# Left-over rows of two heads side by side in the matrix array, in an attention and mixer kernel with a planned order

## The chip, the core and the metric

The kernel runs on one core of one Trainium2 chip. Its metric is the device time of one execution in microseconds. The engines are TensorE (PE; its weight loads are listed apart as PEld), VectorE (DVE), ScalarE (ACT), GpSimd (POOL) and SyncE (SP), which here only issues transfers. Each engine works through its own queue in order, and waits for the others by semaphores.

## The reference

Attention over 4 batches, 8 heads, 576 rows and 64 columns a head, with a bias computed from row and column numbers, then a token mixer and a channel mixer on the result:

```
scores = (1/8) q @ k^T + bias            # bias[h,i,j] from log1p(|i-j|) / log1p(max(i,1)) through a 32-wide layer
attn   = exp(scores - max) / (sum + 1e-9)
x      = (attn @ v), heads side by side  # 4 x 576 x 512
u      = x + (relu(x^T @ w_tok1) @ w_tok2)^T
out    = u + relu(u @ w_ch1) @ w_ch2
```

## The kernel before

Numbers of high precision are split into a high and a low half, and a product is made of three: high x high, high x low, low x high. The program has three stages.

1. The bias table is computed (products of `mm`, L521, overwritten to SBUF by `over`, L526) and written to DRAM in 36 pieces.
2. Sixteen units follow, each one pair of heads (`hp`, 4) of one batch (`b`, 4), in the order of the list `units`. A unit has five query chunks (`c`). Chunks 0 to 3 hold 128 rows of one head after the other; chunk 4 holds the left-over 64 rows of both heads, the first head on partitions 0 to 63 and the second on 64 to 127. For each chunk: `scores` (L799; in chunks 0 to 3 the two heads run on the two row halves of the array), `biased` (L808, bias and maximum on VectorE), `numer` (L821, exponential on ScalarE), then the transposition of the result, by TensorE (`flip`, L850, with halves by L853 and L856) or, for the first third of chunks 0, 2 and 4, by a transposing transfer from SP (`turn`, L839), ahead of which ScalarE makes the high half (`rest_hi`, L831) and GpSimd the low (`rest_lo`, L835 and L389). `back` (L877 to L879) multiplies with v: 30 matmuls of 64 or 65 columns a chunk, the 65th being the sum. `norm1` to `norm3` (L889, L892, L902) divide by the sum. After the chunks `mix1` and `mix2` (L921 to L932) do the token mixer for that pair, and the rows are stored to DRAM (L950 for chunks 0 to 3, L952 for the left-over rows).
3. The channel mixer reads the rows back: first-layer products (L1112 to L1114), second-layer products (L1203 to L1205) and, for the later blocks, products of sums of quarters (L1297 to L1299).

In chunk 4 before, each transposed block has 128 columns, of which 64 are wanted. So the transposed tiles have margins of 64 zero columns on both sides (cleared by `fillt`, L619), the weights are read 64 columns to the left or right, and each of the two heads' results lands on all 128 partitions, of which the half for that batch (`r`) is kept. Even batches use the upper half of a shared tile of left-over rows, odd ones the lower, so the mixer's weights for the last rows (`wt1`) are laid out twice.

What sets the order: nothing is issued in the order of the source. Every step is added to a `Plan` with its possible engines and their costs in microseconds, a due time (from the table `DUE`) and the steps it follows. `Plan.order` simulates the engines with these costs and takes, of the steps that could start first, the one due earliest. `wire` costs stand for transfers; `LAT["D"]` is added behind one. Where TensorE would stand still for over `GAP`, warming matmuls (`keep_warm`, L323; 128 weight columns, 256 columns, result unused) are written ahead of the waiting step, as many as fit in the planned gap at 0.11 each. The queue of each engine is the order in which the plan issues.

The bias of a head pair is read back chunk by chunk (`bias_load`, L725 and L728) into one of two slots. The reads for pairs 2 and 3 overwrite those of pairs 0 and 1, and wait for all `biased` steps of that pair.

Of the kernel before, what the change touches and what calls it, by code (L numbers as in the profile page):

```python
# [56 lines left out]
ON = {'dlo': {'P': 1.9},  # L57
      'dlo2': {'P': (1.9, 2361.48), 'V': (0.67, 1106.04)},
      'late': {'P': (0.7, 2182.65), 'A': (0.58, 1929.34)},
      'klow': {'P': (1.5, 725.99), 'V': (0.83, 1661.39)},  # L60
      'zlow': {'P': (1.25, -2146.14), 'V': (0.6, 1553.62)},
      'twhole': {'P': (2.4, -4606.89), 'V': (1.21, -877.53)},
      'tsum': {'P': (3.0, 1929.59), 'V': (1.72, -1684.06)},
      'tlow': {'P': (2.1, 1515.55), 'V': (1.15, 1987.78)},
      'oall': {'P': (2.7, 2055.41), 'V': (1.2, 3109.89)},
      'norm': {'V': (0.35, -1885.6), 'A': (0.88, -688.24)},
      'over': {'A': 0.65, 'V': (0.72, 542.69)},
      'vh': {'P': (0.7, 5132.87), 'V': (0.4, -2850.86), 'A': (0.6, -3115.7)},
      'vl': {'P': (1.36, 3857.78)}}
DUE = {'tie': 5203.01,  # L70
       'blk': -1054.62,
       'blkn': 61.65,
       'rect': -611.01,
       'bmm': -2320.58,
       'over': -3195.14,
       'put': -4039.31,
       'bl': -239.81,
       'bln': 58.76,
       'sums': 1668.2,
       'sumsn': 550.06,  # L80
       'measw': 331.87,
       'measwn': 95.35,
       'amax': 338.6,
       'scales': 76.3,
       'scalet': -3035.39,
       'scalec': -965.86,
       'fill': -1626.0,
       'fill1': 540.27,
       'tok': -1994.09,
       'tokn': -250.04,  # L90
       'dec1': -350.27,
       'dec2': 379.95,
       'dec3': -1095.12,
       'dec4': 826.35,
       'dec5': -740.87,
       'load_k': -384.96,
       'load_q': -892.85,
       'split_k': -249.75,
       'first_k': 530.16,
       'first_q': 277.17,  # L100
       'split_q': -616.87,
       'load_v': -2393.38,
       'prep_v': 4942.17,
       'prep_vh': -1513.45,
       'prep_vl': -5395.73,
       'scores': -1907.38,
       'biased': -476.81,
# [1298 lines left out]
```

## Time and profile before

| | us |
|---|---|
| median of 3 runs (627.15 to 627.92) | 627.87 |
| the profiled execution | 630.01 |
| its span, first to last instruction | 627.4 |
| PE busy in the span (98%) | 613.2 |
| DVE busy (77%) | 480.0 |
| ACT busy (65%) | 406.9 |
| POOL busy (48%) | 301.1 |

Matmuls are pipelined: one lasts longer than the distance to the next one's start, so TensorE's busy time counts overlaps once and says little about how dense it is. The distance between starts says more. The stages are, by the lines that run in them: the bias table to about 55 us, the units to about 358 us (first `scores` at 54, last `mix2` at 358), the channel mixer from 350 us to the end.

### The profile page before, as it was taken

What the parts mean: (1) busy time and instruction counts of PE and PEld (TensorE: products, weight loads), DVE (VectorE), ACT (ScalarE), POOL (GpSimd) and SP (SyncE); (2) the same over time, 40 slices, a digit from 0 to 9 for tenths busy, and PEclk for the clock granted to TensorE, in tenths of its full rate; (3) what the DMA queues carried; (4) which work ended last, traced back from release to release, by engine and by line L of the source; (5) the groups of instructions that cost most, each with busy time, mean ns of one, the idle gap of its engine ahead of it and who ended that gap; (6) DMA issues with size and microseconds to landing.
All of it is one profiled execution on the core that took longest, in us unless ns stands there. A gap on an engine that the chain in (4) does not pass through costs nothing.

```text
span 627.4 us, 18139 instructions
## 1 busy us (share of the span) xinstructions
PE 613.2 (98%) x7237; PEld 452.3 (72%) x7237; DVE 480.0 (77%) x1188; ACT 406.9 (65%) x751; POOL 301.1 (48%) x343
## 2 busy tenths in 40 slices
PE   9999998999999999999999999999999999999997
PEld 4346776989988998899898964444444468845886
DVE  7897898988899998998999868985764884355322
ACT  7998887988898899999897535543533641234110
POOL 0006789886686888978665510002335742212211
PEclk9999997999999999999999999999999999999999
DMA  8999778999897965658447999544123015400221
GB/s 311 367 387 357 188 159 193 284 263 217 186 247 208 247 145 142 151 128 203 106 91 134 207 351 241 201 134 135 35 67 93 9 34 135 101 1 1 85 85 33
DMA packets 102339, 104.53 MB, mean 167 GB/s; under 512 B 62192, under 2 KB 71920, under 8 KB 102256
## 3 DMA queue, kind: packets, MB, share of 16 engines
q1 hardware_dynamic: 92608, 82.79, 50.2%
q10 hardware_dynamic: 9648, 20.60, 11.3%
q8 instruction: 56, 0.92, 0.6%
q14 instruction: 27, 0.22, 0.1%
HBM read 68.88 MB, written 20.33 MB: 142 GB/s over the span
## 4 chain that ended last, share of the span: by engine, by line
PE 77%; DVE 8%; ACT 7%; DMA 4%; POOL 2%; issue 2%; ACTq 0%; SPq 0%; POOLq 0%; DVEq 0%
PE pair L799 9%; PE bank L850 7%; PE bank L1112 5%; PE bank L1114 5%; PE bank L1113 5%; PE bank L1299 4%; PE bank L1298 4%; PE bank L1297 4%; PE pair L521 4%; PE pair L1113 2%; PE bank L1205 2%; PE pair L1114 2%; PE bank L1204 2%; PE pair L1112 2%; PE bank L1203 2%; PE bank L877 2%
## 5 line engine op out<-in xcount | busy, mean ns | idle before, releaser
L821 ACT ACTIVATE z<-z,mx 128x576 f32<-128x576 f32 (+1 forms) x119 | 91.1, 778 | 9.4 <-DVE mx L808 8.4
L808 DVE CUSTOM_DVE_ANT_0 z<-pair,slots 128x576 f32<-128x576 f32 (+1 forms) x119 | 89.0, 757 | 6.1 <-PE pair L799 5.5
L856 DVE SCALAR_TENSOR_TENSOR t2a<-bank,t2a 128x384 f16<-128x384 f32 (+1 forms) x134 | 70.8, 536 | 8.2 <-ACT t2a L853 7.3
L850 PE MATMUL bank<-id,z 128*128 128x128 f32 x425 | 68.4, 283 | 2.3 <-ACT z L821 1.0
L853 ACT ACTIVATE t2a<-bank 128x384 f16<-128x384 f32 (+1 forms) x134 | 62.7, 471 | 9.5 <-PE bank L850 5.2
L799 PE MATMUL pair<-kh,qh 64*128 64x288 f32 (+1 forms) x288 | 61.5, 349 | 4.2 <-DVE mx L808 3.7
L1112 PE MATMUL bank<-slots 128*128 128x512 f16 (+1 forms) x168 | 58.6, 349 | 0.0
L1113 PE MATMUL bank<-slots 128*128 128x512 f16 (+1 forms) x168 | 58.6, 349 | 0.0
L1114 PE MATMUL bank<-slots 128*128 128x512 f16 (+1 forms) x168 | 58.6, 349 | 0.0
L1308 DVE SCALAR_TENSOR_TENSOR slots<-bank,crow,slots 128x256 f32<-128x256 f32 x42 | 19.5, 481 | 49.7 <-PE bank L1299 36.2
L877 PE MATMUL bank<-vh,t2a 128*128 128x65 f16 x472 | 53.6, 194 | 0.0
L850 PEld LDWEIGHTS bank<-id,z 128*128 128x128 f32 x425 | 45.7, 141 | 10.8 <-issue 3.4
L878 PE MATMUL bank<-vl,t2a 128*128 128x64 f16 x472 | 53.3, 191 | 0.0
L879 PE MATMUL bank<-vh,t2a 128*128 128x65 f16 x472 | 53.3, 192 | 0.0
L799 PE MATMUL pair<-kl,qh 64*128 64x288 f32 (+1 forms) x288 | 52.1, 301 | 0.0
L799 PE MATMUL pair<-kh,ql 64*128 64x288 f32 (+1 forms) x288 | 50.5, 294 | 0.0
L1242 POOL TENSOR_TENSOR me<-me 128x512 f32<-128x512 f16 x12 | 13.6, 1154 | 68.7 <-DVE wd L1088 68.4
L799 PEld LDWEIGHTS pair<-kh,qh 64*128 64x128 f32 (+1 forms) x288 | 33.9, 187 | 15.5 <-issue 6.4
L877 PEld LDWEIGHTS <-t2a 128*128 128x128 f16 x472 | 43.4, 97 | 0.5 <-issue 0.5
L878 PEld LDWEIGHTS <-t2a 128*128 128x128 f16 x472 | 43.6, 98 | 0.2
L879 PEld LDWEIGHTS <-t2a 128*128 128x128 f16 x472 | 43.4, 97 | 0.0
L1320 POOL TENSOR_TENSOR slots<-slots 128x1024 f32<-128x1024 f32 x6 | 14.1, 2350 | 56.5 <-DVE slots L1308 44.6
(272 smaller groups left out, 2131.9 us busy)
## 6 DMA issues: line engine op xcount, KB each, us to landing
keep<-wc SPq DMA_DIRECT2D x24, 512.0 KB, 4.4
wd<-wc SPq DMA_DIRECT2D x24, 512.0 KB, 5.0
bd<-slots SPq DMA_DIRECT2D x36, 295.5 KB, 6.2
slots<-bd SPq DMA_DIRECT2D x16, 576.0 KB, 7.2
tv<-v ACTq DMA_DIRECT2D x16, 320.0 KB, 3.9
qq<-qT ACTq DMA_DIRECT2D x16, 320.0 KB, 3.6
kk<-kT ACTq DMA_DIRECT2D x16, 320.0 KB, 3.9
z<-vr SPq DMA_DIRECT2D x8, 576.0 KB, 7.3
```

Source lines behind the costliest of these rows:

```text
L799: PE.matmul(out=pairs[both[h].i][:, 512 - i + n * i:512 + n * i], lhsT=qx[x][w, c * 128:c * 128 + 128], rhs=kx[y][w, k0:k0 + i], start=(j ...
L808: V.tensor_tensor_reduce(out=st["z"][z.i][:, o], in0=pairs[ph.i][:, 512 - i:512 + i], in1=bias_m[hp][:, c, h, :] if c < NCH else bias_l[hp ...
L821: A.activation(out=zz, in_=zz, func=ACTF.Exp, bias=mx_t[z.i][:, h:h + 1], scale=-1.0)
L850: PE.transpose(banks[tb.i][:, n * 128:(n + 1) * 128], st["z"][z.i][:, 384 * i + n * 128:384 * i + (n + 1) * 128], id32)
L853: A.activation(out=block(h.i, 0, m), in_=banks[tb.i][:, 0:128 * m], func=ACTF.Copy, scale=P_SCALE)
L856: V.scalar_tensor_tensor(out=block(h.i, 3, m), in0=banks[tb.i][:, 0:128 * m], scalar=P_SCALE, in1=block(h.i, 0, m), op0=ALU.mult, op1=ALU. ...
L877: PE.matmul(out=o, lhsT=lh, rhs=vh[:, n, 0:D + 1], start=(i == 0), stop=False)
L878: PE.matmul(out=ps[:, h, 0:D], lhsT=lh, rhs=vl[:, n, :], start=False, stop=False)
L879: PE.matmul(out=o, lhsT=ll, rhs=vh[:, n, 0:D + 1], start=False, stop=(i == 4))
L1112: PE.matmul(out=ps, lhsT=w[0][:, c], rhs=uh[:, c], start=(c == 0), stop=False)
L1113: PE.matmul(out=ps, lhsT=w[0][:, c], rhs=ul[:, c], start=False, stop=False)
L1114: PE.matmul(out=ps, lhsT=w[1][:, c], rhs=uh[:, c], start=False, stop=(c == 3))
```

## The change

- Chunk 4's product with v: `back` now loads 64 weight columns for each head and writes the first head's rows to partitions 0 to 63 and the second's to 64 to 127 of the same columns; the matmuls of the two heads alternate. The planner's cost for it goes from 0.917 to 0.52.
- The margins of the transposed tiles and their fills go (tiles of 768 instead of 896 columns). Left-over rows of both heads stand on a block diagonal of the x tile, scaled by two instructions (`norm4`) instead of one, stored by two transfers of 64x64 instead of one of 64x128. `wt1` has five blocks instead of six, with the last rows' weights on both partition halves, so its third piece is 256 words wide instead of 512. `wt2`'s last 64 columns are copied once (`twice`) instead of cleared.
- A read of a chunk's bias for pairs 2 and 3 waits for that chunk's `biased` steps only.
- Planned costs of transfers rise (`LAT["D"]` 0.4 to 0.6, k and q 1.06 to 1.25, v 1.18 to 1.4, bias 1.9 to 2.3 behind the first pair, stores 0.75 to 1.1). `GAP` falls from 1.0 to 0.6, warming matmuls are also written where no bank is idle, and `STAY`, `SLACK` and all due times change. `rest_lo` may also go to VectorE; the plan leaves all 48 on GpSimd.

```diff
-LAT = {"V": 0.15, "A": 0.16, "P": 0.08, "T": 0.2, "D": 0.4, "-": 0.0}
-GAP, PAD, PAD_MOST = 1.0, 0.11, 24
-SLACK = 0.096
-STAY = 1604.78
+LAT = {"V": 0.15, "A": 0.16, "P": 0.08, "T": 0.2, "D": 0.6, "-": 0.0}
+GAP, PAD, PAD_MOST = 0.6, 0.11, 24
+SLACK = 0.116
+STAY = 796.12
...
-DUE = {'tie': 5203.01,
-       'blk': -1054.62,
+DUE = {'tie': 4998.17,
+       'blk': -647.68,
...
-                if t - at["T"] > GAP and idle:
-                    s.pad = min(PAD_MOST, int((t - at["T"] - 0.3) / PAD)), min(idle)[1]
+                if t - at["T"] > GAP and (idle or any(h.kind == "pair" for h in s.take)):
+                    s.pad = min(PAD_MOST, int((t - at["T"] - 0.25) / PAD)), min(idle)[1] if idle else None
...
-        fillt = add({"P": 2.6}, DUE["fill1"], lambda e: [G.memset(t[:, a:a + 64], 0.0) for t in st["t2a"] + st["t2d"] for a in (0, 832)], after=[drawn])
...
-            after = [] if hp == 0 else [*bias_all, *wt_s] if hp == 1 else last_use[hp - 2]
-            mask = add({"P": 0.2}, t0, mask_out(hp), after=after)
+            def after(c):
+                return [] if hp == 0 else [*bias_all, *wt_s] if hp == 1 else last_use[hp - 2, c]
+
+            mask = add({"P": 0.2}, t0, mask_out(hp), after=after(NCH))
...
-                    blk = ([(n, n) for n in range(5)], [(n + 1, n) for n in range(4, 9)]) if c < NCH else [[(n + 5 * h, n) for n in range(5)] for h in range(2)]
-                    for h in range(2):
-                        for i, (n, t) in enumerate(blk[h]):
-                            d = 64 * (h - b % 2) if c == NCH else 0
-                            lh, ll = (tt[t][:, y[t] + d:y[t] + d + 128] for y in (th, tl))
-                            o = ps[:, h, 0:D + 1]
-                            PE.matmul(out=o, lhsT=lh, rhs=vh[:, n, 0:D + 1], start=(i == 0), stop=False)
-                            PE.matmul(out=ps[:, h, 0:D], lhsT=lh, rhs=vl[:, n, :], start=False, stop=False)
-                            PE.matmul(out=o, lhsT=ll, rhs=vh[:, n, 0:D + 1], start=False, stop=(i == 4))
+                    if c < NCH:
+                        turns = [[(h, n + h, n, slice(0, 128), i)] for h in range(2) for i, n in enumerate(range(4 * h, 4 * h + 5))]
+                    else:
+                        turns = [[(0, n + 5 * h, n, slice(64 * h, 64 * h + 64), n) for h in range(2)] for n in range(5)]
+                    for turn in turns:
+                        for x, y, d in ((th, vh, D + 1), (th, vl, D), (tl, vh, D + 1)):
+                            for h, n, t, w, i in turn:
+                                PE.matmul(out=ps[w, h, 0:d], lhsT=tt[t][:, x[t] + w.start:x[t] + w.stop], rhs=y[:, n, 0:d],
+                                          start=(i == 0 and x is th and y is vh), stop=(i == 4 and x is tl))
...
+                def norm4(e, hb=hb, hr=hr):
+                    for h in range(2):
+                        q = slice(64 * h, 64 * h + 64)
+                        xo, ps, rc = st["x"][xh_.i][q, 4, q], av_of(hb)[q, 2, 0, 0:D], rc_t[hr.i][q, 2, 0]
+                        if e == "A":
+                            A.activation(out=xo, in_=ps, func=ACTF.Copy, scale=rc)
+                        else:
+                            V.tensor_scalar(out=xo, in0=ps, scalar1=rc, scalar2=None, op0=ALU.mult)
```

Three places show how the queues move. On TensorE, chunk 4 of the first unit's product with v (`rect` and `t2a` hold transposed blocks, `vh` and `vl` the halves of v). Before:

```order
L877 LDWEIGHTS rect_123
L877 MATMUL bank1_67<-vh0_111,rect_123 128x65
L878 LDWEIGHTS rect_123
L878 MATMUL bank1_67<-vl0_112,rect_123 128x64
L879 LDWEIGHTS rect_123
L879 MATMUL bank1_67<-vh0_111,rect_123 128x65
```

After:

```order
L889 LDWEIGHTS rect_123
L889 MATMUL bank0_66<-vh0_111,rect_123 64x65
L889 LDWEIGHTS rect_123
L889 MATMUL bank0_66<-vh0_111,rect_123 64x65
L889 LDWEIGHTS rect_123
L889 MATMUL bank0_66<-vl0_112,rect_123 64x64
L889 LDWEIGHTS rect_123
L889 MATMUL bank0_66<-vl0_112,rect_123 64x64
```

The count of matmuls stays 30; each writes 64 partitions instead of 128, and neighbours are now the same term of the two heads. With this TensorE changes the shape of its tiles 171 times in the whole program, 140 times before.

On GpSimd, the stretch ahead of the first low halves (L835 and L389 before, L846 and L391 after; L733 and L737 are the first of two fills of the bias mask). Before:

```order
L733 MEMSET slots 64x64
L734 MEMSET slots 64x64
L647 TENSOR_TENSOR slots<-keep 128x288
L389 TENSOR_TENSOR kl_108<-kk,kh_107 128x640
L641 TENSOR_SCALAR keep<-keep 128x288
L439 MEMSET vh_111 128x10
L440 MEMSET vh_111 64x1
L441 MEMSET vh_111 64x1
L619 MEMSET t2a_90 128x64 x2
...
L619 MEMSET rect 128x64 x10
L835 TENSOR_SCALAR rect<-rect 128x384
L389 TENSOR_TENSOR rect<-rect 128x384
```

After:

```order
L737 MEMSET slots 64x64
L738 MEMSET slots 64x64
L846 TENSOR_SCALAR z_121<-z_121 128x384
L391 TENSOR_TENSOR rect<-z_121,rect 128x384
L441 MEMSET vh_111 128x10
L442 MEMSET vh_111 64x1
L443 MEMSET vh_111 64x1
```

The low halves move ahead of a split of k, two steps of weight decoding and three fills; the 22 margin fills are gone.

On TensorE, the end of the first run of first-layer products in the channel mixer (L1114 before, L1135 after) and the first second-layer product (L1203 before, L1224 after). Before:

```order
L1113 LDWEIGHTS slots
L1113 MATMUL bank_68<-slots 128x512
L1114 LDWEIGHTS slots
L1114 MATMUL bank_68<-slots 128x512
L1203 LDWEIGHTS slots
L1203 MATMUL bank_69<-me,slots 128x512
```

After:

```order
L1135 LDWEIGHTS slots
L1135 MATMUL bank_67<-slots 128x512
L325 LDWEIGHTS ones_74
L325 MATMUL bank_69<-ones_74 128x256
...
L1224 LDWEIGHTS slots
L1224 MATMUL bank_69<-me,slots 128x512
```

Ten warming matmuls (L325) stand between them. In the whole program there are 148 instead of 85; 18 of either number stand at the start. Of the rest, 67 before and 81 after stand before the last scores of the fourth unit; after that, before has none, and after has 36 in four groups (13, 4, 6 and 13) before the last scores of the fifth unit, 3 in the fourteenth, and these ten.

## Rows read from the trace of the kernel before

**Rows 1.** Busy us (instructions) of each engine by stretch, then clock, DMA share, GB/s.

```profile
55.00:100.00 45.00, 40.35 (x524) 33.51 (x524) 40.87 (x113) 37.40 (x69) 35.82 (x66) 0.99 0.83 206
100.00:160.00 60.00, 59.38 (x938) 54.03 (x939) 51.81 (x138) 51.04 (x99) 46.45 (x55) 0.95 0.97 250
160.00:345.00 185.00, 182.79 (x3168) 166.42 (x3168) 170.11 (x454) 165.76 (x312) 140.23 (x149) 1.00 0.71 164
...
375.00:627.40 252.40, 247.91 (x1523) 148.86 (x1521) 150.28 (x320) 89.91 (x165) 61.55 (x42) 1.00 0.31 88
```

**Rows 2.** Timeline of PE, 205 to 206.6 us: start, us, line, operation, tiles, count.

```profile
205.30 0.29 PE L799 MATMUL pair<-kl,qh 64*128 64x288 f32 x2
...
205.83 0.29 PE L799 MATMUL pair<-kh,ql 64*128 64x288 f32 x2
206.05 0.55 PE L850 MATMUL bank<-id,z 128*128 128x128 f32 x3
206.44 0.19 PE L877 MATMUL bank<-vh,rect 128*128 128x65 f16 x1
206.47 0.20 PE L878 MATMUL bank<-vl,rect 128*128 128x64 f16 x1
```

**Rows 3.** Stretches as in rows 1, around the fall of the clock.

```profile
92.00:99.00 7.00, 5.04 (x67) 3.76 (x65) 6.62 (x22) 5.52 (x11) 6.58 (x7) 1.00 0.71 131
99.00:106.00 7.00, 6.46 (x32) 5.03 (x31) 4.82 (x15) 5.43 (x11) 6.38 (x9) 0.51 1.04 241
```

**Rows 4.** Timeline of PE in the token mixer's first product, 207.7 to 208 us.

```profile
207.71 0.22 PE L921 MATMUL bank<-xh,wt1h 128*128 128x128 f16 x1
...
207.99 0.22 PE L923 MATMUL bank<-xh,wt1l 128*128 128x128 f16 x1
```

**Rows 5.** DVE groups by form: busy us and mean ns of one, then idle before.

```profile
L902 DVE TENSOR_TENSOR x<-bank,rc 64x128 f32<-64x128 f32 x16 | 4.5, 284 | 0.1
...
L889 DVE TENSOR_SCALAR rc<-bank 128x4 f32<-128x4 f32 x16 | 2.4, 153 | 0.3
```

**Rows 6.** Issues of line 952 on SP: ns minimum, median, maximum, first and last start.

```profile
L952 SPq DMA_DIRECT2D ul<-x x16: 461/474/552, 121.9 to 360.6; - x16
```

**Rows 7.** Timeline of POOL ahead of the first transposing transfer.

```profile
59.61 1.05 POOL L619 MEMSET t2a<- 128x64 f16 x12
...
62.02 0.92 POOL L389 TENSOR_TENSOR rect<-rect 128x384 f16<-128x384 f32 x1
```

**Rows 8.** The chain that ended last, 62 to 68 us: start, us, what.

```profile
62.97 4.64 DMA rect<-rect
```

**Rows 9.** The same chain at other places, merged pieces, in order of time.

```profile
55.97 2.18 PE bank L323 x19
...
100.99 1.90 PE pair L799 x6
102.89 1.73 PE bank L323 x8
104.62 1.64 PE pair L799 x12
...
159.63 0.93 PE pair L799 x6
...
209.54 0.55 PE bank L850 x5
...
228.00 0.99 PE pair L799 x12
```

**Rows 10.** Timelines of DVE and of PE at the first second-layer product.

```profile
399.78 0.74 DVE L659 SCALAR_TENSOR_TENSOR me<-wd,sc,me 128x512 f16<-128x512 f32 x1
...
400.36 0.38 PE L1203 MATMUL bank<-me,slots 128*128 128x512 f16 x1
```

**Rows 11.** Timeline of PEld in the bias stage, 49.3 to 51 us.

```profile
49.54 0.30 PEld L521 LDWEIGHTS pair<-slots 128*32 128x32 f32 x20 [0.30 <-issue]
50.15 0.13 PEld L521 LDWEIGHTS pair<-slots 128*32 128x32 f32 x4 [0.30 <-issue]
```

More of the change, by code (lines that the diff above doesn't have):

```diff
@@ new lines @@
+DUE = {'tie': 4998.17,
+       'blk': -647.68,
+       'blkn': 79.22,
+       'rect': -763.01,
+       'bmm': -2389.2,
+       'over': -4044.78,
+       'put': -4260.31,
+       'bl': 687.35,
+       'bln': 124.96,
+       'sums': 2272.7,
+       'sumsn': 556.43,
+       'measw': -241.54,
+       'measwn': 92.23,
+       'amax': -141.77,
+       'scales': -970.88,
+       'scalet': -3014.61,
+       'scalec': 772.49,
+       'fill': -404.22,
+       'fill1': 1011.38,
+       'tok': -2233.95,
+       'tokn': -164.97,
+       'dec1': -585.91,
+       'dec2': -380.29,
+       'dec3': -392.21,
+       'dec4': 699.42,
+       'dec5': -1407.03,
+       'load_k': -1264.93,
+       'load_q': -1001.19,
+       'split_k': -1147.47,
+       'first_k': 1410.2,
+       'first_q': 232.19,
+       'split_q': -402.69,
+       'load_v': -3735.76,
+       'prep_v': 4016.62,
+       'prep_vh': -2553.8,
+       'prep_vl': -4781.38,
+       'scores': -1500.38,
+       'biased': -1240.21,
+       'exp': 519.27,
+       'hi': 533.73,
+       'lo': 972.63,
+       'turn': -190.87,
+       'flip': -1140.85,
+       'fliphi': -1951.26,
+       'flip2': -1141.38,
+       'fliplo': 936.49,
+       'back': 600.3,
+       'norm': -1082.88,
+       'mix0': -1335.11,
+       'mix1': -205.71,
+       'relu': -6606.92,
+       'mix2': -4026.09,
+       'mix2b': -234.02,
+       'store': -125.27,
+       'w1': 1709.14,
+       'w1n': 166.52,
+       'U0': 2578.51,
+       'U0n': -582.54,
+       'U1n': -95.1,
+       'U1': 2259.35,
+       'U2': -1637.7,
+       'Un': 36.54,
+       'U3': 2477.65,
+       'U4': -2877.49,
+       'u1': 4361.86,
+       'u2': -1921.15,
+       'u3': -275.58,
+       'u4': -48.29,
+       'u5': 764.07,
+       'G': 2604.87,
+       'G0': 1101.84,
+       'G0n': 138.28,
+       'g1': -3213.41,
+       'g2': 1156.61,
+       'ur': -60.29,
+       'H': 4157.9,
+       'e1': -456.52,
+       'e2': -4056.91,
+       'e3': 1090.96,
+       'e4': 480.31,
+       't2': 1312.25,
+       't3': 6.7,
+       't4': 631.82,
+       'T1': -1272.87,
+       'Tn': -1.35,
+       'rd': 628.59,
+       'urs': 789.77,
+       'un': -139.24,
+       'v1': -136.69,
+       'v2': 5966.57,
+       'v3': -590.31,
+       'v4': 4843.9,
+       'v5': 1879.7,
+       'v6': 1191.78,
+       'v7': 857.25,
+       'v8': -1948.99,
+       'w2m': -953.59,
+       'w2mn': 105.51}
@@ L1346, in attention_mixer @@
             if s.pad:
[L1347 removed]
+                keep_warm(pairs[0][:, 0:192] if s.pad[1] is None else banks[s.pad[1]], s.pad[0])
             n = nc.n_instructions()
```

213 lines of the change are left out of this document (62 added, 151 removed).

## The prediction

> **What bounds the kernel now.** I read the busy times by stage first [rows 1]. From 375 us to the end TensorE runs a dense stream of long products, and the reader should see that nothing else is near it: VectorE is busy 150.28 of 252.40 us, ScalarE 89.91. Those products exist in the same number after the change, so the end moves only by what the attention stage before it gives or takes, and by what is put between the dense products. In the attention stage no engine is alone. From 160 to 345 us TensorE shows 182.79 of 185 us, but its matmuls overlap in the pipeline, so that figure alone proves little; the starts of neighbours [rows 2] lie as close as they ever do, and that is the better sign. VectorE has 170.11 us there, 92%, ScalarE 165.76, 90%. So TensorE is the first limit and VectorE is 8% behind. From 55 to 100 us TensorE has real holes (40.35 of 45 us), and right after them the granted clock falls to 0.51 [rows 3], which is the 1.2 GHz level.
>
> The profiled execution took 630.01 us, 2.6 more than its span of 627.4; the median of the runs is 627.87. I make the sum inside the span and take it off the median.
>
> **Part 1: left-over rows of two heads side by side.** A unit (one head pair of one batch) has five query chunks; the fifth holds 64 left-over rows of each of two heads. Its product with v is 30 matmuls of 64 or 65 columns before and after; now each loads 64 weight columns, and the two heads' matmuls stand in pairs on the two halves of the array. Before, starts are 0.03 us apart [rows 2], so 30 of them take 0.90 us. The trace has no pair of column halves. The nearest is the scores' pair on two row halves: 288 columns twice, four starts of pairs in 0.53 us, 0.13 each. What would 288 columns cost alone? Matmuls of 128 columns start 0.056 us apart (five in 0.28 [rows 4]) and those of 65 at 0.03, so 0.41 ns a column, and 288 come to 0.12 us; a pair costs some 0.01 us more than one pass. I take 0.040 us for a pair of 65, so 15 pairs are 0.60 us. The array also has to change its shape on the way in and out. Out of the scores' row halves the next start comes 0.22 us later where 0.13 is usual [rows 2], so 0.09 a change, 0.18 for both. Together 0.78 against 0.90: 0.12 us a unit, **1.9 us less** over 16 units. The ends: a pair for the price of one pass (0.030) gives 0.63 and 4.3 us less; halves that don't overlap (0.060) give 1.08 and 2.9 us more. I stay near the row halves because they are the only pairs of large tiles here; both ends stay for the range.
>
> **Part 2: the work beside it.** VectorE's scaling of these rows was one instruction on 64x128 (0.284 us) and becomes two on 64x64 from PSUM. The same kind on four columns takes 0.153 [rows 5]; halfway between the two is 0.22, so 0.44 against 0.284: 0.16 us a unit, 2.5 us in all. VectorE has 8% to spare, and only where it has none does this count: I charge a third, **0.8 us more** (0 to 2.5). The reciprocal loses a column, the last addition works on 128 partitions instead of 64: the partitions work at once, so nothing. Each unit stores its left-over rows by two transfers instead of one: one more issue on SP, about 0.47 us [rows 6], 16 times; the kernel reads those rows back only in the dense stage, and SP waits for data between its issues, so nothing, unless a transpose queued behind the store is what TensorE waits for.
>
> **Part 3: fills that go.** Before, GpSimd cleared the margins of the transposed tiles, 22 fills of which 12 take 1.05 us, 1.9 us together, just ahead of the first low halves [rows 7]; those end at 62.94 us, and the first transposing transfer of the chain starts at 62.97 and holds it for 4.64 us [rows 8]. Now GpSimd does the low halves directly behind the mask fills. What could be late next is ScalarE's high half and VectorE's scale for v, busy in the same moments, so I take **1.0 us less** (0 to 1.8).
>
> **Part 4: the slow clock.** After the holes of 92 to 99 us (TensorE busy 5.04 of 7) the granted clock is 0.51 from 99 to 106 us [rows 3]. Six scores matmuls took 1.90 us there against 0.93 later, twelve 1.64 against 0.99, eight warming matmuls 1.73 where 19 took 2.18 at full clock (0.115 each) [rows 9]: 2.5 us lost. The new order writes 81 warming matmuls into the first four units instead of 67 and in more places, because a gap of 0.6 instead of 1.0 in the planner's count now gets them; so the long hole is less likely. I take **2.0 us less** (2.5 less, or 2.5 more if a second slow stretch appears).
>
> **Part 5: bias reads, dearer transfers, new order.** Reads of the third and fourth head pair may start chunk by chunk. The trace shows no TensorE wait for them in the steady stage, which is dense from 100 us on [rows 1], so nothing. The new costs and due times move nearly everything; the engine that does each kind of work stays the same. One place I can price: ten warming matmuls now stand between the last first-layer product and the first second-layer product of the dense stage. Before, the matmul there starts at 400.36 us without a hole, and the low half of the fourth weight block, wanted nine products later, began on VectorE at 399.78 [rows 10]: little slack. Ten times 0.115 is **1.1 us more**; if the weights are later still, that wait is already in it.
>
> The sum: -1.9 + 0.8 - 1.0 - 2.0 + 1.1 = -3.0 us, so 627.9 - 3.0 = **624.9 us**.
>
> **The rivals.**
> (a) The warming matmuls become the wait (slower). After the fourth unit's scores the new order has four groups of them, 36 in all, where the old had none and TensorE was busy 59.38 of 60 us [rows 1]. With 14 more in the first units and 3 later that is 53, times 0.115: 6.1 us. They are free only while the engine would have stood still. If the transfers come sooner than the planner now believes, they are in the way: 624.9 + 6.1 = 631.0. It turns slower than before once half of them, 3 us, is uncovered. For it: the old trace needed no such gaps. Against it: the other engines work their backlog off meanwhile.
> (b) Loads of 64 columns are slow. A 128-column fp32 load with its transposition takes 0.11 us, five in 0.55 [rows 9]. If a 64-column load goes at that rate, 0.055, and the halves load at once, a chunk is 15 x 0.055 + 0.18 = 1.0 us, 1.7 us more instead of 1.9 less: 628.5. If the halves load one after the other, a chunk is 1.83 us: 641.7. Against the second: 20 loads of 32 columns on column quarters took 0.30 us where four took 0.13, so they start some 0.01 apart [rows 11]. The Trainium skill, TensorEngine Tiling (Array Packing), section Feature Incompatibilities, says column tiling excludes the fast weight load, and its page TensorE: Matmul & The Clock Gate, section LDWEIGHTS, puts a plain load at columns / 1.2 ns, an estimate of 53 ns for 64 columns; by that rule the time is that of the first price. No run yet shows a 64-column fp16 load.
> (c) VectorE becomes the limit. Part 1 then gives nothing and part 2 costs all of its 2.5 us: -1.0 - 2.0 + 1.1 + 2.5 = +0.6, so 628.5. For it: 92% busy; against it: TensorE's holes there are smaller than VectorE's.
> (d) All goes well: pairs at one pass (-4.3), the fills' whole 1.8, the clock's whole 2.5, no charge elsewhere: -8.6, so 619.3.
>
> **How the numbers follow.** Forecast 0.36, (a) 0.18, (b) 0.12 (0.02 of it for the long form), (c) 0.10, (d) 0.24. A measurement of this kernel can tell 0.2%, 1.3 us, from no change: 626.6 to 629.1 counts as the same. The forecast's own range is 622.5 to 627; it gives 0.33 to faster and 0.03 to same. (d) is faster. (b) and (c) lie at the upper edge of the same, 0.12 to it, 0.06 slower, 0.04 faster between their terms. (a) gives 0.03 faster, 0.01 same, 0.14 slower. So faster 0.64, same 0.16, slower 0.20. For 8 in 10 the range goes from 618, a little below (d), to 631, the whole of (a).
>
> **What would show it.** Part 1: starts of the fifth chunk's pairs 0.04 us apart and 0.09 at its edges; 0.06 or 0.11 means (b). Part 3: the first transposing transfer before 62 us. Part 4: a granted clock without a stretch near 0.5. Part 5: the first second-layer product directly behind its warming matmuls. (a) shows as warming matmuls whose next matmul starts without any wait, with its operands long ready; (c) as VectorE without holes in the steady stage while TensorE waits for it. A dense stage of another length, counted from its first product to the end, would make the whole argument wrong.

## The result, and the profile after

The changed kernel takes 631.58 us in the median (630.91 to 631.99) against 627.73; the ratio is 1.0062, interval 1.0049 to 1.0074. I forecast 624.9 (618 to 631) and faster; it is slower by 0.6%. The profiled execution took 631.41 us, its span is 629.6. Of the executions of the kernel before, one took 1006.34 us at a mean granted clock of 0.557 and is left out of every figure here. Engine times of the page, to be held against the table before the change:

```profile
PE 615.1 (98%) x7300; PEld 448.4 (71%) x7300; DVE 481.7 (77%) x1204; ACT 406.1 (64%) x751; POOL 297.6 (47%) x321
```

By stretch, busy us and count of each engine, then clock, DMA share and GB/s, as in [rows 1]:

```profile
55.00:100.00 45.00, 40.91 (x536) 33.74 (x534) 40.04 (x118) 37.95 (x71) 35.94 (x47) 1.00 0.95 244
100.00:160.00 60.00, 59.21 (x957) 52.55 (x954) 52.27 (x142) 49.60 (x93) 40.56 (x49) 1.00 0.97 239
160.00:345.00 185.00, 182.54 (x3186) 163.10 (x3184) 169.82 (x457) 166.16 (x313) 139.72 (x149) 1.00 0.66 154
375.00:629.60 254.60, 249.39 (x1539) 150.06 (x1537) 150.74 (x320) 90.95 (x168) 61.03 (x42) 1.00 0.32 89
```

The reader is to see how little these rows tell. They look like those before, TensorE as busy as ever, and 4 us are gone. Only GpSimd's 40.56 us from 100 to 160 stand out, against 46.45 before. Busy time counts warming matmuls as work, so from here on I count the useful matmuls in a stretch.

The pairs themselves did what was hoped. Timeline of PE in the changed kernel, the fifth chunk of one unit (the answer to [rows 2]):

```profile
201.06 0.55 PE L861 MATMUL bank<-id,z 128*128 128x128 f32 x3
201.54 0.22 PE L889 MATMUL bank<-vh,rect 128*64 128x65 f16 x2
201.59 0.20 PE L889 MATMUL bank<-vl,rect 128*64 128x64 f16 x2
...
202.00 0.20 PE L889 MATMUL bank<-vh,t2a 128*64 128x65 f16 x2
202.13 0.55 PE L861 MATMUL bank<-id,z 128*128 128x128 f32 x3
```

From the first start to the start behind the group it is 0.59 us, where 30 single matmuls took 0.91. In the trace a pair's second matmul starts 0.003 us after its first, and pairs follow each other every 0.032; the first start comes 0.20 after the last transposition where 0.11 is usual, the start behind the group 0.13 after its last instead of 0.03.

The last sign that the prediction named showed too: the dense stage has another length. First products of the dense stage, the kernel before and then the changed one (count, ns minimum, median, maximum, first and last start in us):

```profile
L1112 PE MATMUL bank<-slots x168: 272/379/389, 349.7 to 571.7; 128*128 128x512 f16 x120, 128*128 128x256 f16 x48
L1133 PE MATMUL bank<-slots x168: 272/379/390, 349.7 to 573.5; 128*128 128x512 f16 x120, 128*128 128x256 f16 x48
```

From 349.7 us to the end of the span it is 277.7 us before and 279.9 in the changed kernel. Of these 2.2 us, 1.1 are the ten warming matmuls; 0.7 are a hole at 548 us that the kernel before doesn't have, with a weight load there that waits for its transfer; 0.4 lie behind the last product.

```profile
548.12 0.38 PE L1133 MATMUL bank<-slots 128*128 128x512 f16 x1 [0.34 <-issue]
```

So between these two executions the units differ by 0.4 us only, and the dense stage by 2.2. That is one execution of each; the next section shows how much a stage can differ between executions of one kernel.

### The profile page after: what moved, and what is told of

It is laid out like the page before. It is cut to its first block, busy times and chain, and to the rows that moved or that the text cites. A ratio compares the mean times of both kernels' runs of the same rounds, so it can differ in the third digit from the quotient of the medians.

```text
span 629.6 us, 18331 instructions
## 1 busy us (share of the span) xinstructions
PE 615.1 (98%) x7300; PEld 448.4 (71%) x7300; DVE 481.7 (77%) x1204; ACT 406.1 (64%) x751; POOL 297.6 (47%) x321
## 4 chain that ended last, share of the span: by engine, by line
PE 65%; DVE 7%; POOL 4%; issue 2%; ACT 2%; DMA 0%; ACTq 0%; POOLq 0%; DVEq 0%
PE pair L806 6%; PE bank L1133 5%; PE bank L1134 5%; PE bank L1135 5%; PE bank L889 5%; PE bank L861 4%; PE bank L1319 4%; PE bank L1318 4%; PE bank L1320 4%; PE bank L1224 2%; PE pair L1133 2%; PE pair L1135 2%; PE bank L1225 2%; PE bank L1226 2%; PE pair L1134 2%
## 5 line engine op out<-in xcount | busy, mean ns | idle before, releaser
L829 ACT ACTIVATE z<-z,mx 128x576 f32<-128x576 f32 (+1 forms) x121 | 92.4, 778 | 11.9 <-DVE mx L815 10.6
L815 DVE CUSTOM_DVE_ANT_0 z<-pair,slots 128x576 f32<-128x576 f32 (+1 forms) x121 | 90.4, 758 | 6.2 <-PE pair L806 3.7
L864 ACT ACTIVATE t2a<-bank 128x384 f16<-128x384 f32 (+1 forms) x134 | 62.6, 471 | 14.0 <-PE bank L861 10.2
L1135 PE MATMUL bank<-slots 128*128 128x512 f16 (+1 forms) x168 | 58.6, 349 | 0.0
L889 PE MATMUL bank<-vh,t2a 128*128 128x65 f16 (+1 forms) x944 | 53.9, 194 | 0.0
L889 PE MATMUL bank<-vl,t2a 128*128 128x64 f16 (+1 forms) x472 | 48.6, 192 | 0.0
L889 PEld LDWEIGHTS <-t2a 128*128 128x128 f16 (+1 forms) x1416 | 47.2, 99 | 0.6 <-issue 0.2
L889 PE MATMUL bank<-vh,rect 128*128 128x65 f16 (+1 forms) x656 | 40.7, 195 | 0.0
L1133 PEld LDWEIGHTS <-slots 128*128 128x128 f16 x240 | 23.4, 98 | 23.5 <-issue 0.6
L1135 PEld LDWEIGHTS <-slots 128*128 128x128 f16 x240 | 23.5, 98 | 23.1
```

Source lines behind the costliest of these rows:

```text
L815: V.tensor_tensor_reduce(out=st["z"][z.i][:, o], in0=pairs[ph.i][:, 512 - i:512 + i], in1=bias_m[hp][:, c, h, :] if c < NCH else bias_l[hp ...
L829: A.activation(out=zz, in_=zz, func=ACTF.Exp, bias=mx_t[z.i][:, h:h + 1], scale=-1.0)
L864: A.activation(out=block(h.i, 0, m), in_=banks[tb.i][:, 0:128 * m], func=ACTF.Copy, scale=P_SCALE)
L889: PE.matmul(out=ps[w, h, 0:d], lhsT=tt[t][:, x[t] + w.start:x[t] + w.stop], rhs=y[:, n, 0:d], start=(i == 0 and x is th and y is vh), stop ...
L1133: PE.matmul(out=ps, lhsT=w[0][:, c], rhs=uh[:, c], start=(c == 0), stop=False)
L1135: PE.matmul(out=ps, lhsT=w[1][:, c], rhs=uh[:, c], start=False, stop=(c == 3))
```

## Experiments

Ratios are against the kernel before on the same chip; 0.001 is 0.63 us. "Order held" means that the planner's list of steps, engines and buffers is the same, and only what a step issues differs.

### Does the slow stretch of the clock belong to every execution?

> The kernel before, unchanged, timed against itself, to see the span and the granted clock of its executions one by one. Theory 1 (the stretch at half clock from 99 to 106 us belongs to the one profiled execution of before): most executions have a span near 625.5 us and a mean clock of 0.999, and the median of 627.9 never held the 2 us that I meant to win back. Theory 2 (the stretch is in every execution): spans near 627.4 and a clock of 0.995 throughout.

Measured: 627.62 us, ratio 1.0003 (0.9991 to 1.0014). The profiled execution of this run, around 92 to 106 us, as in [rows 3]:

```profile
92.00:99.00 7.00, 5.00 (x34) 3.37 (x32) 6.27 (x19) 5.49 (x11) 6.49 (x8) 0.84 0.70 174
99.00:106.00 7.00, 7.00 (x72) 5.83 (x72) 5.41 (x16) 5.06 (x11) 6.39 (x10) 0.67 0.89 215
```

The slow stretch is there, at a span of 625.6 us: theory 1 falls as stated, since the 627.4 of the first profile is not the clock's doing. The 1.8 us between these two executions of the same kernel lie nearly all ahead of the units: here the first scores start at 52.4 us, in the first profile at 54.1.

```profile
L799 PE MATMUL pair<-kh,qh x288: 287/390/636, 52.4 to 331.8; 64*128 64x288 f32 x128, 128*128 128x320 f32 x16
```

Single profiles are therefore compared stage by stage below, and the verdicts go by the medians. Of the 111 executions of the kernel before in this study, 36 had a mean granted clock of 0.998 or more and took 627.3 us in the mean; the other 75 took 628.0. The difference is 0.8 us (0.4 either way), and on two of the five chips it is 0.0 and 0.2. This compares executions, not kernels, but it leaves little room for the 2.5 us that I read off the slowed matmuls; and a third of the executions show no such stretch in their mean clock.

### What are the pairs worth, and what the order?

Fifth chunk's product (shortened):

```diff
-  turns = [[(0, n + 5 * h, n, slice(64 * h, 64 * h + 64), n) for h in range(2)] for n in range(5)]
+  turns = [[(h, n + 5 * h, n, slice(0, 128), n)] for h in range(2) for n in range(5)]     # a_serial, ab_serial
```

> The changed kernel with its order held, and the fifth chunk's product with v written as before: full loads of 128 weight columns, one head after the other, no pairs (the sums take one column more; nothing is left out). In the trace of the changed kernel a chunk's 30 matmuls take 0.60 us to the next start and 0.09 more on the way in, against 0.91 before. Theory P (TensorE sets the pace of the units): 16 x 0.22 = 3.5 us slower, 635.1. Theory Q (other engines set it, and TensorE's gain lies beside their waits): within 0.7 us of 631.6.

Measured: 634.41 us, 1.0104 (1.0085 to 1.0122), 0.0042 or 2.6 us above the changed kernel. Theory P, in the main: of the 3.5 us that the pairs save on TensorE (0.22 a unit), about three quarters reach the end.

The next two kernels exchange work and order. The list of steps that the planner makes for one kernel is written into the other (shortened). It fixes the sequence, the engine and the buffers of every step, and where warming matmuls stand; "order" means all of these here, 63 more warming matmuls included:

```diff
-  for s in plan.order():
+  for i, e, pad, takes, behind in ORDER:      # as planned for the other kernel
+      s = plan.steps[i]
+      s.engine, s.pad, s.behind = e, pad, None if behind is None else plan.steps[behind]
+      for h, x in zip(s.take, takes):
+          h.i = x
```

> The changed kernel's work (pairs, two scalings, two stores of left-over rows, no margin fills) issued in the order of the kernel before, with its engines, its buffers and its 85 warming matmuls; the copy of the mixer weights' last columns stands behind the last weight split on GpSimd. Theory O (the new order costs the time, the new work gains it): 627.6 less the 2.8 us that the pairs are worth in a_serial, so about 625, faster than both kernels. Theory S (the new work itself costs more than it gains: 16 more scalings of 0.28 us on VectorE are 4.5 us): 628 to 631.

> The work of the kernel before (full-width products, one scaling, one store, the 22 margin fills ahead of the first low halves) issued in the order of the changed kernel, with its engines, buffers, 148 warming matmuls and its bias reads chunk by chunk. Theory O: the time of a_serial, 634.4, less what the second scaling costs and with the margin fills on top, so 633 to 635. Theory S: within 1 us of 627.6, as the old work is what is quick.

> As ab_order, with the fifth chunk's product written as full loads of 128 columns, one head after the other. Theory P (a pair's gain lies on the path in either order): 2.8 us over ab_order, as a_serial is over the changed kernel. Theory Q (in the old order other engines take the gain): within 0.7 us of ab_order.

Measured, as median and ratio with its interval:

| | order of before | order of the changed kernel |
|---|---|---|
| old work | 627.7 (the kernel before) | ba_order: 635.59, 1.0128 (1.0107 to 1.0149) |
| new work | ab_order: 627.59, 0.9998 (0.9984 to 1.0013) | 631.58, 1.0062 (1.0049 to 1.0074) |
| new work, no pairs | ab_serial: 629.30, 1.0024 (1.0010 to 1.0039) | a_serial: 634.41, 1.0104 (1.0085 to 1.0122) |

This table carries the verdict. The new order costs 4.0 us with the new work and 8 with the old. The new work in the old order costs nothing and gains nothing: the pairs give 1.6 us there (between theories P and Q of ab_serial; the two intervals touch), and something in the rest takes them back. Theory O was right that the order is what costs, but not in its 625, and ba_order came out just above its 633 to 635; theory S had a share, but 627.6 lies below its 628.

Where the 4.0 us lie between the two kernels of the new work, in one execution of each (ab_order, then the changed kernel; first scores and first products of the dense stage, columns as above):

```profile
L869 PE MATMUL pair<-kh,qh x288: 287/350/417, 54.1 to 330.8; 64*128 64x288 f32 x128, 128*128 128x320 f32 x16
L1196 PE MATMUL bank<-slots x168: 269/379/391, 347.3 to 570.1; 128*128 128x512 f16 x120, 128*128 128x256 f16 x48
```

```profile
L806 PE MATMUL pair<-kh,qh x288: 287/350/416, 53.7 to 336.7; 64*128 64x288 f32 x128, 128*128 128x320 f32 x16
L1133 PE MATMUL bank<-slots x168: 272/379/390, 349.7 to 573.5; 128*128 128x512 f16 x120, 128*128 128x256 f16 x48
```

The units take 293.2 us in ab_order and 296.0 in the changed kernel, 2.8 more; the dense stage 278.5 (its span is 625.8) and 279.9, 1.4 more, of which the ten warming matmuls are 1.1. So in these executions the order costs 2.8 us in the units, for which the prediction has no term. A hole at the place of that at 548 us stands in the profiles of a_norm1, a_serial and ba_order too, and not in those of ab_order, ab_serial and ab_diag.

### The rest of the new work: the second scaling

> The changed kernel, order held, with one scaling of 128x64 for the left-over rows instead of two of 64x64 (it leaves out putting them on the block diagonal). In the trace of the changed kernel one takes 0.280 us, so 16 x 0.28 = 4.5 us of VectorE go. Theory V (VectorE sets the pace of the units): 2 to 4.5 us faster, 627 to 629.5. Theory O (waits between the queues set it): within 0.7 us of 631.6.

One scaling for both heads, which leaves the block diagonal out (shortened):

```diff
-  for h in range(2):
-      q = slice(64 * h, 64 * h + 64)
-      xo, ps, rc = st["x"][xh_.i][q, 4, q], ...
+  for h in range(1):
+      q = slice(0, 128)
+      xo, ps, rc = st["x"][xh_.i][q, 4, 0:64], ...
```

Measured: 629.71 us, 1.0034 (1.0013 to 1.0054), 1.8 us below the changed kernel. DVE group of the scaling in the changed kernel (busy us, mean ns of one):

```profile
L927 DVE TENSOR_SCALAR x<-bank,rc 64x64 f32<-64x64 f32 x32 | 9.0, 280 | 0.2
```

Two of these stand where [rows 5] has one of 284. I had taken 0.22 each. Of the 4.5 us that VectorE saves in a_norm1, 1.8 reach the end: just short of theory V's 2, and its interval overlaps the changed kernel's a little, but far from theory O's 0.7. A version of ab_order that computes everything replaces the two by one product with a mask (shortened; the sequence of instructions is ab_order's, a few steps use another buffer of the same kind):

```diff
+  V.scalar_tensor_tensor(out=x[:, 4] as (2, 64), in0=ps[:, 2, 0:1, 0:D].to_broadcast([128, 2, D]),
+                         scalar=rc[:, 2, 0], in1=ones on the block diagonal, op0=ALU.mult, op1=ALU.mult)
```

> As ab_order, but the left-over rows of both heads are scaled and put on the block diagonal by one VectorE instruction on 128x128 (the product with the row's ratio and with a mask of ones and zeros) instead of two of 64x64. If one takes about 0.30 us as 64x128 did before, 16 x 0.26 = 4.2 us of VectorE go. Theory V (VectorE's time is on the path): 1.5 to 2.5 us less than ab_order, 625 to 626. Theory O: within 0.7 us of ab_order, 627.6.

```profile
L1030 DVE SCALAR_TENSOR_TENSOR x<-bank,rc,both 128x128 f32<-128x128 f32 x16 | 5.5, 343 | 0.0
```

Measured: 626.08 us, 0.9973 (0.9957 to 0.9988). It is below both kernels, by 1.6 us below ab_order's ratio (the intervals touch), for 16 x (0.56 - 0.34) = 3.5 us of VectorE.

### Where the new order loses: the warming matmuls?

Both kernels of this pair do the same work, so their stretches can be compared. 114 to 134 us, first ab_order (old order), then the changed kernel; columns as above:

```profile
114.00:124.00 10.00, 9.58 (x142) 8.96 (x141) 8.27 (x19) 8.59 (x18) 9.02 (x12) 1.00 1.12 234
124.00:134.00 10.00, 9.90 (x195) 8.72 (x193) 9.36 (x26) 8.62 (x17) 7.85 (x9) 1.00 1.10 293
```

```profile
114.00:124.00 10.00, 9.78 (x121) 8.56 (x120) 8.68 (x23) 6.89 (x12) 6.17 (x9) 1.00 1.16 214
124.00:134.00 10.00, 10.00 (x162) 8.38 (x161) 7.93 (x22) 8.10 (x15) 5.13 (x6) 1.00 0.80 175
```

TensorE looks busier in the new order, but the three engines that it feeds did less: together 51.7 us of 60 in the old, 42.9 in the new. The matmuls of that stretch by line (busy us and count; then clock, DMA share, GB/s) tell what TensorE did. Scores, transpositions and products with v in ab_order:

```profile
114.00:134.00 20.00, 5.18 (x54) 1.00 1.11 263
114.00:134.00 20.00, 6.08 (x39) 1.00 1.11 263
114.00:134.00 20.00, 4.94 (x150) 1.00 1.11 263
```

The same three and the warming matmuls (L325) in the changed kernel:

```profile
114.00:134.00 20.00, 8.23 (x78) 1.00 0.98 195
114.00:134.00 20.00, 4.17 (x30) 1.00 0.98 195
114.00:134.00 20.00, 2.64 (x90) 1.00 0.98 195
114.00:134.00 20.00, 3.03 (x23) 1.00 0.98 195
```

The new order runs the fifth unit's scores there, 78 instead of 54, and has fewer transpositions and products with v to set between them; 23 warming matmuls fill the gaps. The chain that ended last goes through them:

```profile
122.03 0.73 DVE z L815
...
122.82 1.06 PE pair L806 x11
123.88 1.53 PE bank L325 x13
125.41 1.04 PE pair L806 x12
126.45 0.54 PE bank L325 x4
```

That looks as if they were in the way, as rival (a) said. Leaving them out (order held):

```diff
-  if s.pad:
+  group += bool(s.pad)
+  if s.pad and not (12 <= group <= 15):      # a_pad36; a_pad49: group >= 12
       keep_warm(...)
```

> The changed kernel with its order held, and only the 36 warming matmuls of the fifth unit (groups of 13, 4, 6 and 13 between 122 and 135 us) not written. Theory A (they are the wait: the matmul behind them had its operands ready): the time falls by up to 36 x 0.115 = 4.1 us, from 631.6 to about 627.5, and the granted clock stays at 1.00. Theory B (they fill a wait that other engines impose, or what they cost is given back later by VectorE or GpSimd): 631.6, within 0.7. Theory C (they keep the clock up): the time stays or rises, with a stretch near 0.5 after 122 us.

> As a_pad36, and the three warming matmuls of the fourteenth unit and the ten ahead of the first second-layer product are left out too. Theory A: another 1.1 to 1.4 us less than a_pad36, about 626.3. Theory B: the product behind the ten waits for its weights instead, and the time is that of a_pad36.

Measured: a_pad36 630.41 us, 1.0046 (1.0028 to 1.0063); a_pad49 630.41, 1.0034 (1.0020 to 1.0048). By the ratios a_pad36 gets back 1.0 of 4.1 us (-0.3 to 2.4), a_pad49 1.8 of 5.6 (0.6 to 2.9). Timeline of PE in a_pad36 (in brackets: idle before, and for whom); the wait at 121.28 is in the changed kernel too, 0.22 us at 122.82, but at 123.16, 123.84 and 137.47 TensorE now waits where warming matmuls stood:

```profile
121.28 0.40 PE L806 MATMUL pair<-kh,qh 64*128 64x288 f32 x1 [0.24 <-DVE mx L815]
...
123.16 0.40 PE L806 MATMUL pair<-kh,qh 64*128 64x288 f32 x1 [0.83 <-DVE mx L815]
123.84 0.39 PE L806 MATMUL pair<-kh,qh 64*128 64x288 f32 x1 [0.28 <-DVE mx L815]
...
137.47 0.22 PE L942 MATMUL bank<-xl,wt1h 128*128 128x128 f16 x1 [1.45 <-POOL xl L391]
```

A chunk's scores write two pairs of banks, and the next chunk's must wait until VectorE has read both. With nothing else in TensorE's queue between two chunks it waits for VectorE, and at 137 us for GpSimd. The changed kernel at the same two places, the first product with v behind the scores and the mixer's product that waited for GpSimd, and then a_pad36's first product with v and its stretch from 124 to 134 us:

```profile
126.83 0.19 PE L889 MATMUL bank<-vh,rect 128*128 128x65 f16 x1
138.09 0.22 PE L942 MATMUL bank<-xl,wt1h 128*128 128x128 f16 x1
```

```profile
125.21 0.23 PE L889 MATMUL bank<-vh,rect 128*128 128x65 f16 x1
124.00:134.00 10.00, 9.81 (x144) 8.22 (x144) 7.25 (x20) 7.88 (x16) 5.93 (x6) 0.83 0.64 152
```

From the scores at 122.82 (121.28 in a_pad36) to the product with v it is 4.01 us with the first 17 warming matmuls and 3.93 without: that is theory B. From there to the mixer's product it is 11.26 with the other 19 and 12.26 without. The clock fell there, and the products with v from 125.21 take 2.92 us where the changed kernel's take 1.82, so theory C has a part in this execution; but two executions of a_pad36 with a mean clock of 1.00 took 630.0 and 630.4. The span of a_pad36 is 1.0 us shorter all the same, but not by this stretch: its first scores start 1.6 us earlier, at 52.1, and it lacks the hole at 548 us. The ten ahead of the first second-layer product were in the way as forecast (in the changed kernel they start at 400.41 and the next product at 401.50; in a_pad49 it follows without a hole), though 0.8 us between the ratios of a_pad36 and a_pad49 is within their intervals. The 14 more in the first four units were never left out.

### Late transfers?

In the same stretch three transposing transfers take 8.4 to 10.7 us to land. Three runs ask whether that starves TensorE.

> The changed kernel with one stretch of TensorE's queue altered: the two products with v of the third unit's third and fourth chunk stand ahead of the fifth unit's second scores instead of behind them, and the 13 + 4 warming matmuls between 123.8 and 127 us are not written; all else is held. Theory M (the queue's order there is what made TensorE wait): the products fill the 1.5 us in which VectorE reads the scores' banks, and the time falls by 1 to 1.9 us, to about 630. Theory T (the products wait for their transposing transfer, which takes 8 us to land there): TensorE waits in front of the products instead, with the wait named on the transfer, and the time is 631.0 to 632.

Measured: 630.68 us, 1.0060 (1.0037 to 1.0083): no gain by the ratio. Moved ahead, the product does wait for its transfer:

```profile
124.05 0.20 PE L993 MATMUL bank<-vh,rect 128*128 128x65 f16 x1 [1.71 <-DMA rect<-rect]
```

That is theory T for the moved place; it doesn't say that the transfer was late for the old one.

> a_pad36 (the changed kernel, order held, without the fifth unit's 36 warming matmuls) with only half of the partitions of the second pair's bias read for chunks 0 to 3 (rows 64 to 127 are left at zero), so 4 x 288 KB less are moved between 104 and 115 us. In the traces a transposing transfer behind these reads takes 8 to 12 us to land, and TensorE's next product waits for it (in a_swap until 124.0 us). Theory T (the transfers crowd there): the transposing transfers land in 4 to 6 us, TensorE's waits between 115 and 137 us shrink, and the time falls 2 to 4 us below a_pad36, to 626.5 to 628.5. Theory M (the queues' order alone): landing is quicker, but the time stays within 0.8 us of 630.4.

> The same halving of the second pair's bias reads in ab_order, the changed work in the order of before. Theory T: there a transposing transfer lands in 6 us behind the same reads and TensorE was dense, so little is won, under 1 us: 626.6 to 627.6. If this falls as far as a_half does against a_pad36, the reads cost both orders the same and don't explain why the new one is slower.

Measured: a_half 631.97, 1.0073 (1.0060 to 1.0086); ab_half 629.35, 1.0029 (1.0017 to 1.0041). Both rose by 1.7 to 1.9 us, because GpSimd now writes the zeros at the start, 3.93 us in a_half:

```profile
0.72 3.93 POOL L482 MEMSET slots<- 64x4608 f32 x1 [0.29 <-POOLq L1422]
```

TensorE's first bias products wait for GpSimd there until 6.35 us, where those of a_pad36 start at 5.19. And the halving did not do what it was for: the transposing transfers of a_half still took 9.1 to 10.2 us. Inconclusive, since the suspected cause had not been removed. The next one removes it (shortened):

```diff
-  load_words(e, st["raw"][h.i], w1_in[i], 512)
+  load_words(e, st["raw"][h.i], w1_in[i][:, 0:1] if 6 < i < 10 else w1_in[i], 128 if 6 < i < 10 else 512)
   # and the third pair's first bias read stands behind the three transposing transfers
```

> a_pad36 (the changed kernel, order held, no warming matmuls in the fifth unit) with less to move ahead of the three transposing transfers of 113 to 121 us: the third pair's first bias read, which the finer wait had let go ahead of them at 109 us, stands behind them, and the three weight blocks read for their maximum at 104 to 111 us are read to a quarter (128 KB of 512; the rest of their buffers holds the blocks before). That is 1.7 MB less in a crowd in which the transposing transfers took 8.4 to 10.7 us to land. Theory T (TensorE runs dry because these transfers land late): they land in 4 to 7 us and the time falls to 626.5 to 628.5. Theory M (the order of the queues is what starves TensorE, late transfers or not): within 0.8 us of a_pad36's 630.4.

Landing of the three transposing transfers, first in a_pad36, then in a_light:

```profile
L850 SPq DMA_TRANSPOSE rect<-rect x3: 1222/1776/3276, 112.0 to 116.8; - x3
DMA to landing us min/median/max: 8.2/9.3/10.5
```

```profile
L954 SPq DMA_TRANSPOSE rect<-rect x3: 1209/1212/1224, 112.0 to 116.3; - x3
DMA to landing us min/median/max: 2.8/3.0/4.2
```

They land 6 us sooner, and the time is 630.42 us, 1.0033 (1.0018 to 1.0047), by the ratios 0.8 us below a_pad36, within the intervals. The 2 to 4 us of theory T are not there; 0.8 is the edge of theory M. The wait for GpSimd at the mixer's product ends at 137.41 us in a_light and at 137.47 in a_pad36: in the queues as the new order has them, the transfers were not what TensorE waited for there.

### Can the loss be cut out of the order?

> The changed kernel's work in a mixed order: as the changed kernel issues it up to the sixth unit's last token-mixer product (near 194 us), from there as the kernel before does (with neither the later three nor the ten warming matmuls). In the traces of the changed kernel and of ab_order, which do the same work, the same point of TensorE's work is reached 3.7 us later at 194 us and 2.4 us later at 344 us. Theory E (the first six units in the new order make the loss): 627.6 + 3.7 = about 631. Theory L (the loss lies in the rest, or grows evenly): 627.6 to 628.5.

> The opposite mixture: the order of the kernel before up to the sixth unit's last token-mixer product (near 189 us), from there the order of the changed kernel, with its three and its ten warming matmuls. Theory E: the later units are no slower in the new order; 627.6 - 1.3 that they won back in the trace + 1.1 for the ten = about 627.4. Theory L: 630 to 631.

> hba6 with the single scaling of ab_diag and without the three and the ten late warming matmuls. If E and V hold: 627.6 - 1.3 - 1.9 = about 624.4, faster than both kernels. If neither holds: 628 to 630.

Measured: hab6 634.08, 1.0100 (1.0075 to 1.0126); hba6 634.92, 1.0112 (1.0086 to 1.0137); best1 630.97, 1.0064 (1.0041 to 1.0087). Both mixtures are slower than either order, and best1 takes neither the 624.4 nor the 628 to 630; no theory had this. The seam costs more than the stretch that was to be cut out; hba6 at its seam, and ab_order there:

```profile
190.00:200.00 10.00, 6.79 (x59) 5.54 (x57) 6.50 (x22) 5.56 (x10) 5.85 (x9) 0.76 0.70 231
```

```profile
190.00:200.00 10.00, 10.00 (x179) 8.93 (x177) 9.20 (x31) 8.80 (x18) 6.92 (x9) 1.00 0.80 174
```

So these runs don't place the loss. Two more kernels let the planner make new orders:

> The changed kernel's work, ordered by its own planner from the due times, engine costs, transfer costs and gap rule of the kernel before; the warming matmuls that this plan puts behind the fourth unit are left out. Theory D (the dearer transfers and their due times made a worse order): 626 to 628. Theory R (due times fit the work they were chosen with, and any table taken over to other work gives a worse order): 630 to 635, as ba_order showed for the opposite case.

> The changed kernel with the bias reads of the third and fourth pair waiting for all chunks of the pair before last, as they did before; the planner then orders the work anew from the ninth unit on and, by its look-ahead, partly earlier. If the finer wait is worth something, it is slower than 631.6 by more than 1 us; theory R says that an order not chosen for it may be slower too, and a time within 1 us of 631.6 says that the finer wait is worth nothing.

Measured: a_oldtab 653.91, 1.0429 (1.0398 to 1.0461); a_waitall 635.52, 1.0128 (1.0102 to 1.0153). Theory D falls, but a_oldtab lies as far beyond theory R's 630 to 635. The old tables under the new work are 26 us worse than the old order itself under the new work (ab_order), and in its profile the loss lies in the dense stage: it lasts 310.6 us from its first product at 346.0, against 279.9 in the changed kernel. TensorE waits there for up to 9.22 us at a time (until 504.92, for ScalarE), and the mean granted clock is 0.55 to 0.60 from 500 to 512 us. Why this plan is so bad is not shown; that tables serve only the work that they were chosen with remains a guess. a_waitall changes the order too, so what the finer wait is worth by itself stays open.

## Why the prediction was wrong, step by step

- **Part 1 had the mechanism right and the size a little low.** 1.9 us were forecast; taking the pairs away costs 2.6 us in the new order and 1.6 in the old. A pair came at 0.032, close to the price of one pass (0.030), below the 0.040 that I took; the edges cost 0.09 and 0.10 as forecast. So TensorE saves 3.5 us, but not all of it reaches the end: that the forecast came close is in part luck. Rival (b), loads of 64 columns at 0.055, falls.
- **Part 2 was mis-sized.** A scaling of 64x64 takes 0.280, not 0.22, so VectorE got 4.5 us more, not 2.5; of these 1.8 reach the end (a_norm1), not 0.8. "Halfway between four columns and 128" was a guess, and its upper end belonged into the range as it stood, 0.284. With this alone parts 1 and 2 cancel, as ab_order shows.
- **Part 3 gained nothing.** The first transposing transfer of the changed kernel does begin at 60.51 us instead of 62.97. But ab_order has no margin fills either, and is no faster than the kernel before. Its first low half is ready two microseconds earlier, and the transfer still starts at 63.42, behind two bias reads in SP's queue (62.08 to 63.25). I had looked for the next limit on ScalarE and VectorE; it was the queue.

```profile
60.05 0.92 POOL L454 TENSOR_TENSOR rect<-rect 128x384 f16<-128x384 f32 x1
```

```profile
63.42 4.99 SPq L913 DMA_TRANSPOSE rect<-rect  x2
```

- **Part 4 took one execution for all.** The clock held in the changed kernel, as forecast. But the credit was 2.0 us where the stretch goes with 0.8 in two executions of three. And I took it off a median that did not carry the 2 us by which the profiled execution was longer: b_again has the same slow stretch and a span of 625.6, and what was longer lies in the bias stage.
- **Part 5 is the step that failed.** "The new costs and due times move nearly everything" stands there, and the sum has no term for it: I priced the one place that I could see, the ten warming matmuls (1.1 us, and right), and the rest of a new order went in at zero, with no reason but that "the engine that does each kind of work stays the same". The order costs 4.0 us with the new work and 8 with the old; about 2.9 of the 4.0 had no term. Which part of the order does it stays open. What the order listing showed, 36 warming matmuls where the old had none, was the planner's own sign that it expected TensorE to wait there. The prediction's last sign, a dense stage of another length, showed as well: 2.2 us more, half of it the ten, the rest not foreseen.
- **Rival (a) had nearly the number, 631.0, and the wrong mechanism.** It took the warming matmuls for the cost. They fill waits that are real: without them TensorE waits for VectorE and GpSimd, and of the 36 about 1 us of 4.1 comes back. That the number came close was luck. The sign that I had set for it, warming matmuls whose next matmul starts without any wait, showed and proves nothing: a filler hides the wait that it fills.
- **Rival (c) was half right.** VectorE's time is on the path (a_norm1, ab_diag), but it does not take the pairs' gain away: that reaches the end in either order. TensorE and VectorE share the path, so a gain on either shows in part.

The sum as measured, against 627.7: new work in the old order 0 (pairs -1.6, the rest +1.6, most of it the second scaling, by a_norm1 and ab_diag), new order +4.0 with its ten warming matmuls: 631.7. Each line of this sum has an uncertainty of about 1 us. That TensorE runs dry between 114 and 137 us is shown by the counts and by the waits of a_pad36; that late transfers there are not the cause is shown by a_light. That the scores placed closely behind each other are the cause is argued from the trace: no run moved them alone, and the stretch is not all of the 4 us, since 1.4 lie in the dense stage of the profiled executions.

## What to carry to other kernels

A change that comes with a new instruction order is two changes. Issue the new work in the old order, and the old work in the new, before pricing either: here the work was worth nothing and the order cost it all, and the same busy shares hid that. Of filler instructions ask what waits when they go: a filler in the critical chain is not yet a cost. And compare two profiles stage by stage, since one execution's length may be set in a stage that the change doesn't touch.

## What the runs showed of the hardware that was not expected

- On column halves two matmuls of 64 or 65 columns start 0.003 us apart, and a pair every 0.032 us with its two loads of 64 columns. The Trainium skill, TensorE: Matmul & The Clock Gate, section LDWEIGHTS, puts a plain load at columns / 1.2 ns, an estimate of 53 ns for 64 columns; the trace doesn't show that price here, a pair with both loads comes in less.
- VectorE's scaling from PSUM takes 0.280 us on 64x64 and, in a_norm1, 0.278 on 128x64; a masked product on 128x128 takes 0.343.
- Reading half of the partitions (288 KB instead of 576) did not land sooner in that traffic: a median of 9.0 us in a_half against 7.7 in the changed kernel. 1.7 MB less of other reads brought the transposing transfers behind them from a median of 9.3 us (a_pad36) to 3.0 (a_light).
